# Batch 0's second round of attention visits as plain fp32 products with TensorE transposes, and the second parts of all weights made by GpSimd

## The chip, the cores and the metric

The kernel runs on one core of one Trainium2 chip. The metric is the device time of one execution in microseconds. Three timed runs of the kernel before took 1231.63 to 1234.51 us, with a median of 1234.36 us. The profile shown here is of another execution, which took 1228.56 us; its span from the first to the last instruction is 1226.8 us.

## The reference

```python
scores = scale * np.matmul(q, k.transpose(0, 1, 3, 2))        # 8 batches, 8 heads, 576 x 64
thresh = np.max(scores, axis=-1, keepdims=True) - tau
scores = np.where(scores >= thresh, scores, -1000000000.0)
scores = scores - np.max(scores, axis=-1, keepdims=True)
attn = np.exp(scores)
attn = attn / (np.sum(attn, axis=-1, keepdims=True) + 1e-09)
x = np.matmul(attn, v)                                         # back to 4608 x 512
h = x @ w_in                                                   # 512 x 2048
g = h * (1.0 / (1.0 + np.exp(-h)))
return g @ w_out                                               # 2048 x 512
```

Attention keeps only the scores that lie within tau of the row's maximum. Its output, with the heads side by side, goes through two large products with a SiLU between them. All inputs are fp32 except the two weight matrices, which arrive as 64-bit floats and are taken apart into words on the chip.

## The kernel before, in words

**Tiles and visits.** The work of attention is cut into tiles of 128 query rows against all 576 keys. A visit is a pair of heads of one batch. For batches 1 to 7 a visit has 9 tiles and covers everything ("all"). Batch 0 is done in two rounds: four "low" visits of 4 tiles each cover 256 query columns (tiles 0 to 15), then, after 12 empty steps, four "high" visits of 5 tiles each cover the other 320 (tiles 28 to 47). Batch 1 begins with tile 49, and the last tile is number 300. One step of the main loop handles one tile and, as a credit allows, one or more units of the two large products ("MoE units" below).

**What a tile does.** `scores` makes the products into PSUM (two buffers of two banks). `soft1` takes the negated maximum on VectorE (L458), `soft1b` the exponential on ScalarE (L468), `soft2` masks and sums on VectorE (L477). `soft2b` multiplies by the reciprocal, and `soft3` brings the tile into the transposed form that the product with v needs.

**Two ways of doing that.** The split way (all visits but the low ones) cuts every operand in two parts so that products of reduced precision add up to fp32: `split_k` (L360 ScalarE, L362 GpSimd), `split_q` (for batch 0 L345 and L346 on ScalarE and L347 on GpSimd, for the others L351 on ScalarE and L352 on VectorE) and `split_v` (L312, L313). A tile's scores are then four matmuls (L448), eight for the tile that two heads share. The scaling is on ScalarE (L495); GpSimd makes two 16-bit parts (L506, L509, L512; up to tile 35 the first one is on ScalarE, L504), a DMA transpose carries them over (L522), and `av` runs 28 16-bit matmuls for each half of a visit (L537). The direct way (the low visits) uses unsplit fp32 q, k and v: two fp32 matmuls a tile (L436, each of them two records in the profile), scaling on GpSimd (L491), five TensorE transposes (L393, L395), two ScalarE copies out of PSUM (L403, L404) and ten fp32 matmuls a visit (L413, two records each).

**The weights.** `load_weights` and `decode_weights` bring in w_in and w_out, 16 tiles each, and rebuild fp32 values (L191 ScalarE, L194 and L197 VectorE). When all 16 tiles of a matrix are decoded a common scale is found, and `split_weights` makes two 16-bit parts: for w_in by GpSimd scaling (L226), a ScalarE copy (L229) and a GpSimd subtraction (L230); for w_out by one ScalarE pass (L221) and one VectorE pass (L222).

**MoE units.** An h unit is 12 matmuls (L580) with a post on ScalarE and VectorE (L588, L589, L595, L596); an o unit is 12 matmuls (L611), four of them to an output tile. Batch 0's units come in two groups, of 256 columns after the low visits and of 320 after the high ones; later batches bring two groups of 288. A group may start only when the attention outputs of all four visits are there. The o units need all of w_out's parts.

**What sets the order.** The Python loop records instructions with priorities (`W_PLAN`, `PRI_*`), and a scheduler that runs when the program is built puts each engine's instructions into one fixed order. On the chip every engine, and the SyncE queue that issues the DMAs, goes through its order without overtaking. Where a group of MoE units stands between two tiles is therefore fixed, whatever the actual times are.

## Time and profile before

| what | value |
|---|---|
| median of 3 timed runs | 1234.36 us |
| profiled execution, its own time | 1228.56 us |
| its span | 1226.8 us |
| first score maximum of tile 28 (first high tile) | 73.38 us |
| first score maximum of tile 49 (batch 1) | 171.70 us |
| first score maximum of tile 95 | 324.32 us |
| TensorE / VectorE / ScalarE / GpSimd busy over the span | 93% / 76% / 66% / 60% |

A tile's place in time is read from its maximum (L458): there is one for each tile, in order, so the 17th is tile 28, the 37th is tile 49 and the 83rd is tile 95. In windows of the trace the clock column is the mean share of full speed that was granted to TensorE. A row of the timeline holds neighbouring instructions of one line, with the start of the first and the time to the end of the last; since matmuls are pipelined, the cost of a row on TensorE is the distance to the start of the next row. Line numbers are those of the kernel before.

### The profile page before, as it was taken

The numbers are of one execution on the slowest core, as the hardware profiler recorded it, in microseconds if no ns is written. First come the engines' busy times: TensorE is split into PE (matmuls) and PEld (weight loads), VectorE is DVE, ScalarE is ACT, GpSimd is POOL, SyncE is SP. The second block draws the span as 40 slices with busy tenths as digits, with TensorE's granted clock in tenths as the row PEclk, the third lists the DMA queues.
The fourth block names the chain that finished last, engine by engine and source line by source line (L and its number), as shares of the span: only waits on it lengthen the run. The fifth ranks groups of instructions, "written<-read, shape, count | busy, mean of one in ns | idle before, by whom it ended". The sixth has DMA issues, their size and how long they took to land.

```text
span 1226.8 us, 26991 instructions
## 1 busy us (share of the span) xinstructions
PE 1145.4 (93%) x9422; PEld 898.1 (73%) x9422; DVE 934.2 (76%) x2619; ACT 808.6 (66%) x1491; POOL 739.4 (60%) x936
## 2 busy tenths in 40 slices
PE   6867679999799999999999999999999999999998
PEld 4545458777677777877777877787778877777777
DVE  6988998987888988988889958887789848332330
ACT  5768876776777767776777747776678747333331
POOL 2289968786778778886888528872778447100000
PEclk9967889999999999999999999999999999999999
DMA  9659658687677777786896447872797346200000
GB/s 296 192 182 235 136 117 171 146 139 148 138 145 144 166 148 145 147 160 149 146 174 141 110 115 138 156 144 82 137 159 150 75 86 113 50 11 15 16 11 25
DMA packets 363480, 158.16 MB, mean 129 GB/s; under 512 B 329552, under 2 KB 338256, under 8 KB 363344
## 3 DMA queue, kind: packets, MB, share of 16 engines
q1 hardware_dynamic: 363344, 156.43, 60.6%
q8 instruction: 75, 1.23, 0.4%
q14 instruction: 61, 0.50, 0.1%
HBM read 66.72 MB, written 9.44 MB: 62 GB/s over the span
## 4 chain that ended last, share of the span: by engine, by line
PE 64%; DVE 16%; DMA 8%; ACT 5%; issue 3%; POOL 2%; SPq 1%; ACTq 0%; POOLq 0%; DVEq 0%
PE o L611 24%; PE h L580 22%; PE s L448 9%; PE a L537 7%; DVE w L477 4%; DVE sm L458 3%; DVE qstack L352 2%; DMA wT<-hl 2%; DMA vraw<-in_vL 2%; ACT w L468 2%; DMA wraw<-in_w_out 2%; ACT w L495 1%; DVE gbuf L596 1%; DMA kd<-in_kT 1%; DVE wst L222 1%
## 5 line engine op out<-in xcount | busy, mean ns | idle before, releaser
L580 PE MATMUL h<-x,wst 128*128 128x288 f16 (+2 forms) x3072 | 429.7, 289 | 15.6 <-DVE gbuf L596 12.0
L611 PE MATMUL o<-gbuf,wst 128*128 128x288 f16 (+2 forms) x3072 | 420.0, 286 | 2.0 <-ACT wst L621 1.9
L580 PEld LDWEIGHTS <-wst 128*128 128x128 f16 x3072 | 292.7, 99 | 105.3 <-issue 26.7
L611 PEld LDWEIGHTS <-wst 128*128 128x128 f16 x3072 | 292.8, 98 | 83.4 <-issue 6.7
L509 POOL TENSOR_TENSOR hl<-w,hl 128x512 f16<-128x512 f32 x272 | 326.4, 1200 | 14.6 <-ACT hl L504 1.2
L506 POOL TENSOR_SCALAR hl<-w 128x576 f16<-128x576 f32 x264 | 179.9, 684 | 202.5 <-ACT w L495 141.2
L468 ACT ACTIVATE w<-s,sm 128x576 f32<-128x576 f32 x288 | 210.9, 737 | 78.9 <-DVE sm L458 33.1
L477 DVE SCALAR_TENSOR_TENSOR w<-s,sm,w 128x576 f32<-128x576 f32 x288 | 232.6, 813 | 35.9 <-ACT w L468 34.0
L458 DVE TENSOR_REDUCE sm<-s 128x1 f32<-128x576 f32 x288 | 215.1, 751 | 41.5 <-PE s L448 32.4
L495 ACT ACTIVATE w<-w,sm 128x576 f32<-128x576 f32 x272 | 205.7, 770 | 49.3 <-DVE sm L485 47.1
L589 DVE SCALAR_TENSOR_TENSOR h<-th,h 128x288 f32<-128x288 f32 (+2 forms) x256 | 116.5, 457 | 109.3 <-ACT th L588 107.2
L588 ACT ACTIVATE th<-h,msc 128x288 f32<-128x288 f32 (+2 forms) x256 | 126.8, 498 | 106.4 <-PE h L580 104.7
L448 PE MATMUL s<-khi,qstack 128*128 128x288 f32 x608 | 160.0, 345 | 27.1 <-DVE w L477 23.4
L595 ACT ACTIVATE gbuf<-h 128x288 f16<-128x288 f32 (+2 forms) x256 | 103.6, 407 | 80.7 <-DVE h L589 79.7
L596 DVE SCALAR_TENSOR_TENSOR gbuf<-h,gbuf 128x288 f16<-128x288 f32 (+2 forms) x256 | 115.4, 453 | 40.1 <-ACT gbuf L595 39.1
L448 PEld LDWEIGHTS s<-khi,qstack 128*128 128x128 f32 x608 | 97.4, 196 | 51.3 <-issue 34.4
L448 PE MATMUL s<-klo,qstack 128*128 128x288 f32 x608 | 133.6, 301 | 0.0
L537 PE MATMUL a<-wT,v 128*64 128x288 f16 (+1 forms) x1680 | 129.7, 293 | 4.0 <-DMA wT<-hl 3.7
L362 POOL TENSOR_TENSOR klo<-kraw,khi 128x576 fp32r<-128x576 f32 x64 | 94.8, 1481 | 43.1 <-ACT khi L360 43.0
L537 PEld LDWEIGHTS <-v 128*64 128x64 f16 x1680 | 92.0, 111 | 31.5 <-issue 22.8
L512 POOL TENSOR_TENSOR hl<-w,hl 128x64 f16<-128x64 f32 x272 | 102.5, 377 | 0.0
L448 PEld LDWEIGHTS s<-klo,qstack 128*128 128x128 f32 x608 | 101.0, 195 | 0.3
(103 smaller groups left out, 831.6 us busy)
## 6 DMA issues: line engine op xcount, KB each, us to landing
qraw<-in_qT SPq DMA_DIRECT2D x128, 144.0 KB, 3.0
kraw<-in_kT SPq DMA_DIRECT2D x128, 144.0 KB, 3.0
vraw<-in_vL SPq DMA_DIRECT2D x32, 320.0 KB, 3.3
wraw<-in_w_out SPq DMA_DIRECT2D x16, 512.0 KB, 4.1
out_t<-wst SPq DMA_DIRECT2D x56, 144.0 KB, 2.2
wT<-hl SPq DMA_TRANSPOSE x304, 3.3
gbuf<-in_w_in SPq DMA_DIRECT2D x8, 512.0 KB, 7.1
wraw<-in_w_in SPq DMA_DIRECT2D x8, 512.0 KB, 6.5
```

What stands on the lines that cost most here:

```text
L448: nc.tensor.matmul(s_ps[:, j, :HALF], lhs, kk[:, j * HALF : (j + 1) * HALF], start=(n == 0), stop=(n == len(seq) - 1),)
L458: nc.vector.tensor_reduce(out=negm, in_=s_ps[:, :, :HALF], op=ALU.max, axis=AX.XY, negate=True)
L468: nc.scalar.activation(wtile[t].rearrange("p (j c) -> p j c", j=2), sps[t][:, :, :HALF], AF.Exp, bias=small[t][:, 0:1],)
L477: nc.vector.scalar_tensor_tensor(out=w3, in0=s_ps[:, :, :HALF], scalar=sm[:, 1:2], in1=w3, op0=ALU.is_ge, op1=ALU.mult, accum_out=sm[:, 2:3],)
L495: nc.scalar.activation(w, w, AF.Copy, scale=r)
L506: nc.gpsimd.tensor_scalar(out=fl[:, 0:S], in0=w, scalar1=1.0, scalar2=1.0, op0=ALU.mult, op1=ALU.mult)
L509: nc.gpsimd.tensor_tensor(out=fl[:, 640:1152], in0=w[:, 0:512], in1=fl[:, 0:512], op=ALU.subtract)
L537: nc.tensor.matmul(a_ps[odd * D : (odd + 1) * D, :n], vt[:, lo_v, odd, kv, :], wT[v, b * H + 2 * p + odd][:, kw, c0 - base : c0 - base + n ...
L580: nc.tensor.matmul(ph[:, :n], wi(c, f, lo_w), x16[b, lo_x][:, c, c0 : c0 + n], start=(k == 0), stop=(k == 11),)
L588: nc.scalar.activation(th[:, :n], ph[:, :n], AF.Tanh, scale=moe_sc[b][:, 0:1])
L596: nc.vector.scalar_tensor_tensor(out=g[:, 1, :n], in0=ph[:, :n], scalar=2.0**-14, in1=g[:, 0, :n], op0=ALU.mult, op1=ALU.subtract,)
L611: nc.tensor.matmul(ps[:, :n], wo(f, d, lo_w), g[:, lo_g, :n], start=(f == 0 and k == 0), stop=(f == NF - 1 and k == 2),)
```

## The change

The high visits of batch 0 now go the direct way too. Their q halves are loaded straight into two more zero-padded tiles, so that batch 0 needs no `split_q`, `split_k` or `split_v` and no DMA transposes. Their transposes use PSUM bank 1 and the bank that the product with v uses; the first group's MoE units take banks 0 and 2. `split_weights` handles w_out as w_in: GpSimd scales, ScalarE copies, GpSimd subtracts. Batch 1's v is loaded and its maximum taken later, and its scale is found four steps later.

```diff
     def split_weights(i):
-        if i >= 4 * NK:
-            nc.scalar.activation(hi, w, AF.Copy, scale=sc)
-            nc.vector.scalar_tensor_tensor(
-                out=w16[:, i, 512:1024], in0=w, scalar=sc, in1=hi, op0=ALU.mult, op1=ALU.subtract
-            )
-            return
         nc.gpsimd.tensor_scalar(
             out=w, in0=w, scalar1=sc, scalar2=1.0, op0=ALU.mult, op1=ALU.mult
         )
...
     def vscale(b):
         vsc[b] = pow2_scales(
-            vmx[b], f"v{b}", (None, 2)[b] if b < 2 else 0, squared=(b == 0)
+            vmx[b], f"v{b}", (None, 1)[b] if b < 2 else 0, squared=(b == 0)
         )
...
     def split_q(h, tiles):
-        if h < H:
-            nc.scalar.activation(src, src, AF.Copy, scale=gate)
-            nc.scalar.activation(dst, src, AF.Copy)
-            nc.gpsimd.tensor_tensor(
-                out=dst[D:P, :], in0=src[D:P, :], in1=dst[D:P, :].bitcast(F32), op=ALU.subtract
-            )
-        else:
-            nc.scalar.activation(dst, src, AF.Copy, scale=gate)
...
+    qzero = {}
+    for kind, base, n in (("low", 4096, 256), ("high", 5120, 320)):
...
     def load_direct(v):
+        qt = qzero[kind, v % 2]
+        n = VISITS[kind][2][0][1]
+        c0, c1 = (0, S - n) if kind == "low" else (S - n, 0)
+        nc.sync.dma_start(out=qt[0:D, 0:n], in_=qT[b, 2 * p, :, c0 : c0 + n])
+        nc.sync.dma_start(out=qt[D:P, n : 2 * n], in_=qT[b, 2 * p + 1, :, c1 : c1 + n])
...
     def soft3_direct(t):
-        main = bank([P, 4, P], f"tm_{t}")
+        main = bank([P, 4, P], f"tm_{t}", None if low else 1)
...
-        last = bank([P, P], f"tl_{t}")
+        if low:
+            last = bank([P, P], f"tl_{t}")
+        else:
+            last = ps_a.tile([P, 512], F32, tag="a", name=f"tl_{t}")[:, 0:P]
...
     def moe_units(b, c0, n):
+        if b == 0 and c0 == 0:
+            return h_units(b, c0, n, (0, 2)) + o_units(b, c0, n, (0, 2))
...
-        if kind == "low":
+        if b == 0:
             at(u - LOAD, lambda v=v: load_direct(v))
             at(u - 2, lambda v=v: scale_direct(v))
...
             if b == 0:
                 at(-4, lambda p=p: load_v(0, p))
                 at(0, lambda p=p: vmax(0, p))
-                at(V_SLOT + p, lambda p=p: split_v(0, p))
+            elif b == 1:
+                at(u + 5 * p - 20, lambda p=p: load_v(1, p))
+                at(u + 5 * p - 15, lambda p=p: vmax(1, p))
+                at(u + 9 * p + 4, lambda p=p: split_v(1, p))
...
-        at(u - 2 if b else 1, lambda b=b: vscale(b))
+        at((1, u + 2)[b] if b < 2 else u - 2, lambda b=b: vscale(b))
```

The order of instructions moves with it. Two places matter below. The first is GpSimd around tiles 41 to 43. In the rows, w32_41 is tile 41's weights after the exponential, hl its two 16-bit parts, klo the second part of k, and wst the MoE weights. Before, GpSimd stood there in the middle of the high tiles:

```order
L509 TENSOR_TENSOR hl_41_1935<-w32_41_1886,hl_41_1935 128x512
L512 TENSOR_TENSOR hl_41_1935<-w32_41_1886,hl_41_1935 128x64
L506 TENSOR_SCALAR hl_42_1983<-w32_42_1925 128x576
L509 TENSOR_TENSOR hl_42_1983<-w32_42_1925,hl_42_1983 128x512
L512 TENSOR_TENSOR hl_42_1983<-w32_42_1925,hl_42_1983 128x64
L362 TENSOR_TENSOR klo_8_2110<-kraw_8_8_2030,khi_8_2108 128x576
```

Now, from tile 38 on, one scaling pass stands for each tile (L488, the former L491), and w_out's scaling (L218, the former L226) and subtractions (L222, the former L230) stand between them:

```order
L488 TENSOR_SCALAR w32_38_1660<-w32_38_1660,sm_38_1659 128x576
L218 TENSOR_SCALAR wst_89<-wst_89,o_w_sc_1020 128x512 x15
L222 TENSOR_TENSOR wst_89<-wst_89 128x512
L218 TENSOR_SCALAR wst_89<-wst_89,o_w_sc_1020 128x512
L222 TENSOR_TENSOR wst_89<-wst_89 128x512
L488 TENSOR_SCALAR w32_39_1712<-w32_39_1712,sm_39_1711 128x576
L488 TENSOR_SCALAR w32_40_1749<-w32_40_1749,sm_40_1748 128x576
L222 TENSOR_TENSOR wst_89<-wst_89 128x512 x2
L488 TENSOR_SCALAR w32_41_1795<-w32_41_1795,sm_41_1794 128x576
```

A tile's three passes have become one, and all sixteen scalings of w_out stand in one row ahead of tile 39's.

The second place is TensorE around tile 85, where batch 2's attention begins. Before, pieces of batch 0's second group of o units (o_0_256) stood between the tiles' scores:

```order
L448 MATMUL s_85_3616<-khi_16_3549,qstack0_85 128x288 x2
L448 MATMUL s_85_3616<-klo_16_3551,qstack0_85 128x288 x2
L611 LDWEIGHTS wst_89
L611 MATMUL o_0_256_2_3594<-gbuf_61,wst_89 128x320
L448 MATMUL s_86_3653<-khi_16_3549,qstack0_85 128x288 x2
L448 MATMUL s_86_3653<-klo_16_3551,qstack0_85 128x288 x2
```

Now the scores of tiles 84 to 89 follow each other with nothing between (L445 is the former L448):

```order
L445 MATMUL s_84_3461<-khi_15_3203,qstack1_87 128x288 x2
L445 MATMUL s_84_3461<-klo_15_3205,qstack1_87 128x288 x2
L445 MATMUL s_85_3514<-khi_16_3435,qstack0_85 128x288 x2
L445 MATMUL s_85_3514<-klo_16_3437,qstack0_85 128x288 x2
L445 MATMUL s_86_3551<-khi_16_3435,qstack0_85 128x288 x2
L445 MATMUL s_86_3551<-klo_16_3437,qstack0_85 128x288 x2
L445 MATMUL s_87_3582<-khi_16_3435,qstack0_85 128x288 x2
L445 MATMUL s_87_3582<-klo_16_3437,qstack0_85 128x288 x2
```

All of batch 0's MoE units now stand ahead of tile 82: the whole first group of o units (192 matmuls) between the scores of tiles 49 and 51, where before none of them stood, and the second group between tiles 51 and 82. From there to tile 95 only 18 MoE matmuls stand on TensorE beside attention's own, where before 230 stood (146 of batch 0's o matmuls and 84 of batch 1's h matmuls).

More of the change, by code (lines that the diff above doesn't have):

```diff
@@ L366, in attention_moe @@
     direct = {}
[L367 to L371 removed]
+    qzero = {}
+    for kind, base, n in (("low", 4096, 256), ("high", 5120, 320)):
+        for i in range(2):
+            t = gbuf.bitcast(F32)[:, base + 2 * n * i : base + 2 * n * (i + 1)]
+            nc.gpsimd.memset(t[0:D, n : 2 * n], 0.0)
+            nc.gpsimd.memset(t[D:P, 0:n], 0.0)
+            qzero[kind, i] = t
     def load_direct(v):
[L374 removed]
+        b, p, kind = visits[v]
         kt = sb.tile([P, S], F32, tag="kraw", name=f"kd_{v}", bufs=2)
         nc.sync.dma_start(out=kt, in_=kT[b, 2 * p : 2 * p + 2].rearrange("h d s -> (h d) s"))
[L377 to L379 removed]
+        qt = qzero[kind, v % 2]
[3 more added lines that the diff above has]
+        nc.sync.dma_start(out=qt[D:P, n : 2 * n], in_=qT[b, 2 * p + 1, :, c1 : c1 + n])
         direct[v] = qt, kt
@@ L383, in scale_direct @@
         for j in range(2):
-            own = direct[v][0][j * D : (j + 1) * D, 256 * j : 256 * (j + 1)]
+            n = VISITS[visits[v][2]][2][0][1]
+            own = direct[v][0][j * D : (j + 1) * D, n * j : n * (j + 1)]
             nc.scalar.activation(own, own, AF.Copy, scale=gate[j * D : (j + 1) * D, :])
@@ L433, in scores @@
             qt, kt = direct[v]
-            o = (h % 2) * 256 + i * P
+            if visits[v][2] == "low":
+                o = (h % 2) * 256 + i * P
+            else:
+                o = (h % 2) * 384 + (i - 2) * P
             for j in range(2):
@@ L502, in soft3 @@
         fl = hl.rearrange("p j c -> p (j c)")
[L503 to L508 removed]
+        nc.gpsimd.tensor_scalar(
+            out=fl[:, 0:S], in0=w, scalar1=1.0, scalar2=1.0, op0=ALU.mult, op1=ALU.mult
+        )
         nc.gpsimd.tensor_tensor(
@@ L644, in moe_units @@
         if held:
-            for pair in zip(h_units(b, c0, n, (0, 1)), o_units(*held.pop(), 2)):
+            for pair in zip(h_units(b, c0, n, (0, 1)), o_units(*held.pop(), (2,))):
                 out.extend(pair)
```

31 lines of the change are left out of this document (8 added, 23 removed).

## The prediction

> **What bounds the kernel now.** I read the windows of the trace by stage first, cut at the score maxima (L458) of tiles 28, 49, 51 and 95; the timeline rows are those of tiles 28, 49, 82 and 95:
>
> ```profile
> 73.38 0.74 DVE L458 TENSOR_REDUCE sm<-s 128x1 f32<-128x576 f32 x1
> 171.70 0.75 DVE L458 TENSOR_REDUCE sm<-s 128x1 f32<-128x576 f32 x1
> 274.18 0.76 DVE L458 TENSOR_REDUCE sm<-s 128x1 f32<-128x576 f32 x1 [0.33 <-PE s L448]
> 324.32 0.75 DVE L458 TENSOR_REDUCE sm<-s 128x1 f32<-128x576 f32 x1
> ...
> core 0: us, PE busy (x) PEld busy (x) DVE busy (x) ACT busy (x) POOL busy (x), PEclk, DMA share, GB/s
> 0.00:73.40 73.40, 53.33 (x296) 34.89 (x296) 57.41 (x179) 47.50 (x90) 21.97 (x31) 0.91 0.77 238
> 73.40:171.70 98.30, 67.66 (x425) 49.75 (x426) 91.15 (x218) 80.01 (x147) 85.33 (x88) 0.74 0.70 172
> 171.70:179.70 8.00, 5.45 (x31) 4.07 (x29) 7.44 (x26) 5.12 (x10) 4.75 (x7) 0.57 0.51 105
> 179.70:324.30 144.60, 134.29 (x1128) 105.26 (x1125) 122.60 (x350) 102.59 (x181) 113.59 (x144) 1.00 0.78 151
> 324.30:500.00 175.70, 166.77 (x1431) 132.17 (x1430) 155.22 (x449) 130.83 (x239) 136.17 (x175) 1.00 0.73 146
> 500.00:1042.30 542.30, 536.78 (x4621) 427.85 (x4619) 449.01 (x1290) 384.10 (x701) 372.02 (x487) 1.00 0.67 132
> ```
>
> After 500 us TensorE is busy 99% of the time at full clock: the kernel is bound by TensorE there, and from 180 us on nearly so. Only ahead of tile 49 is it not. In the high stage (tiles 28 to 49, 98.3 us) VectorE is busy 93%, while TensorE idles for 30.6 us and runs at 0.74 of its clock. So any work added to TensorE is paid at the end, unless time is won in which TensorE now idles or is slowed. The forecast is that balance: work added, lost time recovered, lost time made anew.
>
> Next come the groups of the high stage.
>
> ```profile
> L197 DVE SCALAR_TENSOR_TENSOR wst<-wraw,wst 128x512 int32<-128x512 int32 x12 | 15.2, 1265 | 0.1
> L222 DVE SCALAR_TENSOR_TENSOR wst<-wst,o_w_sc 128x512 f16<-128x512 f32 x14 | 13.6, 993 | 0.0
> L313 DVE SCALAR_TENSOR_TENSOR v<-vraw,v_sc,v 128x640 f16<-128x640 f32 x3 | 3.8, 1254 | 0.0
> L495 ACT ACTIVATE w<-w,sm 128x576 f32<-128x576 f32 x18 | 13.8, 771 | 0.4 <-DVE sm L485 0.3
> L230 POOL TENSOR_TENSOR wst<-wst 128x512 f16<-128x512 f32 x16 | 19.5, 1241 | 0.1
> L362 POOL TENSOR_TENSOR klo<-kraw,khi 128x576 fp32r<-128x576 f32 x8 | 12.0, 1505 | 2.3 <-ACT khi L360 2.3
> L226 POOL TENSOR_SCALAR wst<-wst,i_w_sc 128x512 f32<-128x512 f32 x12 | 9.9, 843 | 0.0
> L491 POOL TENSOR_SCALAR w<-w,sm 128x576 f32<-128x576 f32 x2 | 2.1, 1036 | 0.0
> L580 PE MATMUL h<-x,wst 128*128 128x256 f16 (+1 forms) x160 | 24.9, 304 | 7.7 <-DVE gbuf L596 6.8 <-DVE sm L481 0.9
> ```
>
> L222 and L313, the passes that the change removes from VectorE, are 17.4 us of its 91.15. That speaks for a gain. What replaces them goes to GpSimd, which is already busy for 85.33 us.
>
> **Work added to TensorE.** Prices come from timeline rows at full clock, as the distance to the next row.
>
> ```profile
> 48.98 2.52 PE L413 MATMUL a<-wT,vraw 128*64 128x256 f32 x18
> 51.43 1.24 PE L436 MATMUL s<-kd,gbuf 128*128 128x288 f32 x4
> 52.50 0.62 PE L209 MATMUL wps<-wst 128*128 128x128 bf16 x8
> 52.96 0.60 PE L393 MATMUL tm<-ident,w 128*128 128x128 f32 x4
> 53.40 0.27 PE L395 MATMUL tl<-ident,w 128*128 128x128 f32 x1
> 53.51 1.14 PE L436 MATMUL s<-kd,gbuf 128*128 128x288 f32 x4
> ...
> 137.13 1.47 PE L580 MATMUL h<-x,wst 128*128 128x256 f16 x12 [1.82 <-DVE gbuf L596]
> 138.53 1.14 PE L537 MATMUL a<-wT,v 128*64 128x320 f16 x14
> 139.60 0.54 PE L448 MATMUL s<-khi,qstack 128*128 128x288 f32 x2
> ...
> 247.75 0.54 PE L448 MATMUL s<-khi,qstack 128*128 128x288 f32 x2
> ...
> 248.39 3.43 PE L580 MATMUL h<-x,wst 128*128 128x320 f16 x24
> ```
>
> A split tile's scores, two rows of which the second is left out, cost 0.64 us (247.75 to 248.39), the shared tile's twice that, and half a visit's product with v 2 x 1.07 = 2.14. The four high visits thus cost 16 x 0.64 + 4 x 1.28 + 4 x 2.14 = 24 us of full-clock work. The direct way costs 1.1 us for a tile's scores (51.43 to 52.50 is 1.07), 0.55 for its five transposes (52.96 to 53.51), and for a visit's product 20 records of (2.45/18) x 320/256 = 0.17, so 3.4: 20 x 1.65 + 4 x 3.4 = 47 us. TensorE gets **23 us more**; the records with 320 columns and single gaps could make it 20 to 27, I take 24.
>
> The Trainium skill, in "TensorE: Matmul & The Clock Gate", Part 4 (PE-mode transpose), gives about 275 ns for one 128x128 transpose inside a kernel, which would make the hundred new ones 27 us instead of 11 and the sum 16 us higher. The rows above show four in 0.44 us, 0.11 each, since they follow each other; the measurement decides.
>
> **The low stage.** Batch 0's split_v leaves VectorE (4 x 1.25, with two of batch 1's maxima, less two q parts), and ScalarE and GpSimd no longer hold the low tiles for high q and k. VectorE is the busiest engine there (57.41 of 73.40), and TensorE idles for 20 us. I take **-5 us**; 0 if the weights' loads pace it, -8 at best.
>
> **The high stage.** VectorE: 91 less 13.6, 3.8, two q parts (1.6) and three maxima (2.4), plus 8 more post passes of 0.42, so 73 us. ScalarE: 80 less the scalings (13.8) and the 16-bit copies, k, q and v work (19 together), plus twenty times the two copies out of PSUM (under 0.9 together) and some posts: about 70. GpSimd must, from the first scaling of w_in to tile 49, go through 32 scalings of weights, 32 subtractions, 21 tile scalings and 2 k parts: 32 x 0.843 + 32 x 1.241 + 21 x 1.04 + 2 x 1.5 = 91 us. It begins here:
>
> ```profile
> 69.94 2.19 POOL L226 TENSOR_SCALAR wst<-wst,i_w_sc 128x512 f32<-128x512 f32 x3 [3.28 <-DVE i_w_sc L146]
> ```
>
> With the low stage's 5 us that is 65, so GpSimd is the new bound of the stage and ends at 156 without a wait; with 3 us of waits (for the ScalarE copy between scaling and subtraction, and for w_out's scale, where tiles 39 and on are queued behind the sixteen scalings) tile 49 comes at 159. The stage, from 68 to 159, takes 91 us.
>
> TensorE's full-clock work in it before: 160 h matmuls at 1.40/12 (18.7), 20 tiles of split scores (15.4), three visits' products (6.4), and some 7 of weight maxima and the last low visit: 47, so 51 of 98.3 us were lost. After, by the order: 20 direct tiles' scores (22), 95 transposes (10.5), 40 + 20 product records (9.5), 192 h matmuls (22.4), 4 of weight maxima: 68, so 23 of 91 are lost. Recovered: **28 us**. Between tiles 49 and 51 now stands the o block; TensorE is full there, where 8 us held 4 of work: **-2**.
>
> **What is lost anew.** The order lets batch 0's MoE units run out early. From tile 82 to 95 there is attention alone, and it is paced by the engines behind it, whose prices are those of 500 to 600 us:
>
> ```profile
> L509 POOL TENSOR_TENSOR hl<-w,hl 128x512 f16<-128x512 f32 x31 | 38.3, 1234 | 2.3
> L506 POOL TENSOR_SCALAR hl<-w 128x576 f16<-128x576 f32 x32 | 21.4, 669 | 19.9 <-ACT w L495 17.4 <-ACT th L588 2.5
> L512 POOL TENSOR_TENSOR hl<-w,hl 128x64 f16<-128x64 f32 x31 | 11.7, 378 | 0.0
> ...
> L477 DVE SCALAR_TENSOR_TENSOR w<-s,sm,w 128x576 f32<-128x576 f32 x30 | 24.2, 815 | 4.0 <-ACT w L468 3.9
> L458 DVE TENSOR_REDUCE sm<-s 128x1 f32<-128x576 f32 x32 | 23.9, 751 | 1.8 <-PE s L448 1.7
> ```
>
> GpSimd needs 1.234 + 0.669 + 0.378 = 2.28 us a tile and 0.3 for k; VectorE 1.57 for the two large passes, some 0.6 for the small ones and 0.5 for q, v and maxima: 2.6 to 2.8 us either way, 36 us for 13 tiles. TensorE's work in it is 13 tiles' scores (9.6), one visit's product (4) and 18 MoE matmuls: 15. So 21 us are lost; before, the same tiles took 50 us (274.18 to 324.32), with 230 MoE matmuls for the 18, so 29 us more of work: 6 lost. **+15** (13 to 18). Tiles 51 to 57 are a smaller case: VectorE has six tiles and, moved there, four split_v and five maxima, some 21 us, against 13 of TensorE work; before, 2 were lost. **+6**. From tile 57 to 82, and after 95, TensorE is full as before: -1.
>
> **The sum**, against the profiled execution's own 1228.6 us (1.8 around its span): 24 - 5 - 28 - 2 + 15 + 6 - 1 = **+9 us**, 1237.6. The median shown lies 5.8 us above that execution, so I predict **1243 us**. The price of the transposes and of the direct products is read from the low stage; the least certain term is the stage's length, where 10% is 9 us.
>
> **Rivals.**
> *GpSimd is quick, and it is faster.* L197 costs 0.68 us in the low stage and 1.265 here, so VectorE and GpSimd stretch each other, and VectorE will do less. With the shortest rows of the stage,
>
> ```profile
> 84.68 0.68 POOL L226 TENSOR_SCALAR wst<-wst,i_w_sc 128x512 f32<-128x512 f32 x1
> 39.50 0.68 DVE L197 SCALAR_TENSOR_TENSOR wst<-gbuf,wst 128x512 int32<-128x512 int32 x1
> ```
>
> and 1.14 for the subtraction, GpSimd has 77 us and ends at 142 to 146; the stage loses 10 instead of 23, and the lull at 2.4 us a tile loses 4 less: -8 us, 1226. It decides once the subtraction's mean is under 1.15 us. Against it: GpSimd's load does not fall.
> *The lull is given back, and nothing changes.* The tiles run ahead in it, and in 324 to 500 us TensorE still idles 8.9 of 175.7. If all of that is filled: 0 to +1 us, 1235. Against it: the two PSUM buffers let a tile run only one ahead on TensorE.
> *The clock stays low, and it is much slower.* If the high stage keeps the granted 0.74, 68 us of work take 92, more than the 91 that GpSimd asks for, and with half of the former idle time (15) the stage takes 107: +25 us, 1259. It decides once the clock is under 68/91 = 0.75. For it: 0.57 between tiles 49 and 51 with TensorE 68% busy. Against it: the low stage's second half, at 90% busy with such transposes in it, was at full clock:
>
> ```profile
> 40.00:60.00 20.00, 17.90 (x123) 12.21 (x122) 18.30 (x53) 12.69 (x26) 5.96 (x7) 1.00 0.60 184
> ```
>
> The same Part 4 says that transposes do not count as activity for the clock gate, which would speak for this rival; this row does not bear it out.
>
> **How the numbers follow.** The forecast has 0.45 (its own range 1236 to 1252), the quick GpSimd 0.25, the lull given back 0.15, the low clock 0.15. About 0.3% (3.7 us) is what a measurement of this kernel can tell from no change. Slower takes the low clock and nine tenths of the forecast, 0.55; within it the lull and a tenth of the forecast, 0.20; faster 0.25. The range reaches to most of both sides: 1224 to 1260.
>
> **What would show it.** Tile 49's maximum near 159 us, with GpSimd over 90% busy ahead of it and the clock near 0.9; tile 95's near 335, later than the 324.32 of before though tile 49's is earlier; TensorE idle over half of the time between tiles 84 and 92. If tile 49 comes before 147 or the lull's tiles take under 2.4 us each, the kernel is faster and I am wrong; if TensorE's busy time in the stage is near 90 us at a clock under 0.8, the third rival holds.

## The result, and the profile after

Four runs of the changed kernel took 1249.29 to 1251.13 us, median 1249.75; four of the kernel before on the same chip had a median of 1233.43. The ratio is **1.0152, 95% interval 1.0128 to 1.0175**: the change makes the kernel 1.5% slower, where the forecast was 1243 us. The profiled execution took 1249.85 us and its span is 1248.1. The before profile, 1228.56 us, lies below all of its timed runs, so that the two profiled executions differ by 21.3 us and the medians by 16.3; the stages below are compared between the profiles.

The windows of the changed kernel, cut at the maxima of tiles 28, 49, 51, 57, 82 and 95, then the two parts of the stage from 28 to 49, cut at tile 33. The columns are those of the windows in the prediction.

```profile
0.00:72.60 72.60, 52.27 (x301) 34.24 (x302) 55.41 (x175) 44.36 (x84) 16.59 (x30) 0.93 0.76 235
72.60:164.60 92.00, 73.66 (x479) 52.15 (x479) 69.93 (x192) 65.96 (x147) 76.97 (x84) 0.91 0.28 87
164.60:192.00 27.40, 27.40 (x239) 22.74 (x238) 4.63 (x16) 5.79 (x15) 4.89 (x7) 1.00 0.08 25
192.00:215.50 23.50, 14.50 (x84) 9.54 (x82) 22.99 (x57) 16.36 (x30) 12.25 (x14) 0.80 0.77 172
215.50:300.70 85.20, 80.88 (x651) 60.58 (x651) 73.36 (x217) 60.27 (x106) 65.42 (x84) 0.97 0.69 138
300.70:338.30 37.60, 21.57 (x132) 16.71 (x131) 31.93 (x89) 24.40 (x41) 30.25 (x39) 0.69 0.85 169
500.00:1063.60 563.60, 551.78 (x4740) 440.42 (x4738) 463.48 (x1333) 393.97 (x721) 385.20 (x501) 1.00 0.68 131
...
72.60:103.30 30.70, 19.53 (x95) 11.33 (x95) 22.82 (x50) 16.73 (x31) 26.49 (x29) 0.72 0.53 169
103.30:164.60 61.30, 54.13 (x387) 40.82 (x385) 47.10 (x143) 49.23 (x117) 50.48 (x56) 1.00 0.16 45
```

Tile 49 now comes at 164.6 us instead of 171.7, 7 us early. By tile 51 the kernel is 12 us behind (192.0 against 179.7), by tile 82 26 us (300.7 against 274.2), and at tile 95 14 us (338.3 against 324.3). Two of the rows are stretches in which TensorE is idle and slowed: 23.5 us with 14.5 busy at a clock of 0.80, and 37.6 us with 21.57 busy at 0.69. The kernel before took 17.4 and 50.1 us for the same tiles (51 to 57, and 82 to 95), at full clock and filled with MoE matmuls:

```profile
179.70:197.10 17.40, 16.55 (x150) 14.35 (x148) 15.93 (x43) 12.18 (x23) 15.61 (x20) 1.00 0.79 156
274.20:324.30 50.10, 44.43 (x371) 34.43 (x369) 40.16 (x116) 32.72 (x57) 35.07 (x43) 1.00 0.80 157
```

To set the added work apart from the idle time, I count for each kernel the matmuls that stand in each stretch of TensorE's order, at the prediction's prices at full clock, and call the rest of the stretch lost: idle time, and what a halved clock costs. The sum of the work is 1101 us before and 1125 after. The prices hold in the changed kernel's rows at full clock (18 product records in 2.98 us, a tile's scores in 0.98 to 1.07), but the 24 us are a count at these prices. Counting by start times instead of by the order moves most entries by less than 2 us and some, above all from 51 to 82, by up to 4.5.

| lost time, us | to 28 | 28–33 | 33–49 | 49–51 | 51–57 | 57–82 | 82–95 | after 95 | all |
|---|---|---|---|---|---|---|---|---|---|
| before | 34.2 | 15.6 | 37.1 | 4.0 | 1.7 | 4.8 | 6.0 | 22.8 | 126 |
| after | 32.8 | 18.2 | 7.4 | -0.5 | 11.1 | 7.3 | 23.0 | 24.1 | 123 |

So 33 us of lost time are recovered up to tile 51, 27 of them between tiles 28 and 49, and 30 are lost anew behind it. What stays is the work added, 24 us, less the difference of 3.

### The profile page after: what moved, and what is told of

The parts are those of the page before. It is cut to its first block, busy times and chain, and to the rows that moved or that the text cites. A ratio compares the mean times of both kernels' runs of the same rounds, so it can differ in the third digit from the quotient of the medians.

```text
span 1248.1 us, 26945 instructions
## 1 busy us (share of the span) xinstructions
PE 1160.0 (93%) x9474; PEld 905.3 (73%) x9474; DVE 916.5 (73%) x2599; ACT 792.9 (64%) x1491; POOL 722.1 (58%) x926
## 4 chain that ended last, share of the span: by engine, by line
PE 55%; DVE 16%; DMA 11%; POOL 7%; ACT 6%; issue 6%; SPq 0%; POOLq 0%; ACTq 0%; DVEq 0%
PE o L605 20%; PE h L574 18%; PE s L445 7%; PE a L531 6%; DMA wT<-hl 5%; DVE w L474 4%; DVE sm L455 3%; DVE qstack L337 2%; POOL hl L503 2%; DMA wraw<-in_w_in 2%; POOL hl L500 2%; ACT w L465 2%; DMA vraw<-in_vL 1%; DMA wraw<-in_w_out 1%; ACT w L492 1%
## 5 line engine op out<-in xcount | busy, mean ns | idle before, releaser
L574 PE MATMUL h<-x,wst 128*128 128x288 f16 (+2 forms) x3072 | 427.4, 288 | 12.5 <-DVE x L550 6.0
L503 POOL TENSOR_TENSOR hl<-w,hl 128x512 f16<-128x512 f32 x252 | 302.2, 1199 | 12.2
L500 POOL TENSOR_SCALAR hl<-w 128x576 f16<-128x576 f32 x252 | 170.6, 680 | 225.1 <-ACT w L492 158.9
L474 DVE SCALAR_TENSOR_TENSOR w<-s,sm,w 128x576 f32<-128x576 f32 x288 | 232.9, 813 | 55.7 <-ACT w L465 53.5
L492 ACT ACTIVATE w<-w,sm 128x576 f32<-128x576 f32 x252 | 190.8, 771 | 44.0 <-DVE sm L482 42.0
L445 PE MATMUL s<-khi,qstack 128*128 128x288 f32 x560 | 147.0, 344 | 19.1 <-DVE w L474 13.9
L531 PE MATMUL a<-wT,v 128*64 128x288 f16 x1568 | 118.2, 291 | 10.8 <-DMA wT<-hl 9.8
L445 PE MATMUL s<-klo,qstack 128*128 128x288 f32 x560 | 122.6, 300 | 0.0
L445 PEld LDWEIGHTS s<-khi,qstack 128*128 128x128 f32 x560 | 89.1, 194 | 39.6 <-issue 27.1
L347 POOL TENSOR_TENSOR klo<-kraw,khi 128x576 fp32r<-128x576 f32 x56 | 82.2, 1467 | 39.3 <-ACT khi L345 38.7
L506 POOL TENSOR_TENSOR hl<-w,hl 128x64 f16<-128x64 f32 x252 | 93.0, 369 | 0.0
L445 PEld LDWEIGHTS s<-klo,qstack 128*128 128x128 f32 x560 | 92.4, 193 | 0.5 <-issue 0.2
```

The source lines that it names most:

```text
L445: nc.tensor.matmul(s_ps[:, j, :HALF], lhs, kk[:, j * HALF : (j + 1) * HALF], start=(n == 0), stop=(n == len(seq) - 1),)
L474: nc.vector.scalar_tensor_tensor(out=w3, in0=s_ps[:, :, :HALF], scalar=sm[:, 1:2], in1=w3, op0=ALU.is_ge, op1=ALU.mult, accum_out=sm[:, 2:3],)
L492: nc.scalar.activation(w, w, AF.Copy, scale=r)
L500: nc.gpsimd.tensor_scalar(out=fl[:, 0:S], in0=w, scalar1=1.0, scalar2=1.0, op0=ALU.mult, op1=ALU.mult)
L503: nc.gpsimd.tensor_tensor(out=fl[:, 640:1152], in0=w[:, 0:512], in1=fl[:, 0:512], op=ALU.subtract)
L531: nc.tensor.matmul(a_ps[odd * D : (odd + 1) * D, :n], vt[:, lo_v, odd, kv, :], wT[v, b * H + 2 * p + odd][:, kw, c0 - base : c0 - base + n ...
```

## The experiments

All are compared with the kernel before in runs on the same chip. The order of the instructions is drawn anew for each of them, as it was for the change. Two terms come back: RATES holds the credit for each tile with which batch 0's first and second group of MoE units are drawn, and W_PLAN[0] the steps at which w_in is loaded, scaled and split.

### One part of the change alone

**e1_direct_only** is the change without its second part: w_out's second parts are made by VectorE again.

```diff
         sc = wsc["in" if i < 4 * NK else "out"][:, 0:1]
+        if i >= 4 * NK:
+            nc.scalar.activation(hi, w, AF.Copy, scale=sc)
+            nc.vector.scalar_tensor_tensor(
+                out=w16[:, i, 512:1024], in0=w, scalar=sc, in1=hi, op0=ALU.mult, op1=ALU.subtract
+            )
+            return
```

> The change without its second half: the high visits go the direct way, but w_out's second parts are made by VectorE again, with the ScalarE pass ahead of them. In its order the o units of the first group no longer stand in one block ahead of tile 51 and the stretch with little MoE work is shorter (tiles 85 to 95 hold 1.9 us of TensorE work a tile, against 1.0 to 1.3 in the change). Theory (added TensorE work, plus stretches in which MoE work has run out): TensorE work is as in the change, about half of the lull's 21 us goes, VectorE has 15 us back in the high stage; 1240 us, 1235 to 1246, so between the two kernels. Rival (the weights' move is what helps, the direct visits alone are worse): above 1250 us.

Measured: 1239.25 us (1236.28 to 1241.7), ratio 1.0068 (1.0042 to 1.0095). Two of its windows, tiles 28 to 49 and 82 to 95:

```profile
72.40:167.40 95.00, 73.51 (x458) 50.48 (x458) 79.84 (x205) 66.96 (x144) 53.14 (x55) 0.89 0.27 85
...
294.40:336.70 42.30, 32.48 (x230) 24.65 (x228) 35.08 (x102) 28.04 (x49) 29.77 (x40) 0.88 0.74 151
```

GpSimd has 53.14 us to do in the high stage instead of 76.97, and the stage is not shorter but 3 us longer (95.0). Its length does not follow GpSimd's load, against the prediction. (VectorE, which makes w_out's second parts here, has 10 us more to do, 79.84 instead of 69.93.) The kernel is nevertheless 10 us faster than with the whole change, and that comes from elsewhere: here 189 of the 192 o matmuls stand between tiles 51 and 57, not in one block ahead of 51, and that stretch loses nothing (-0.9 against 11.1); 82 to 95 loses 13.9 against 23.0.

**e2_weights_only** is the kernel before with the other part: the five lines of `split_weights` that take w_out to ScalarE and VectorE are removed.

```diff
-        if i >= 4 * NK:
-            nc.scalar.activation(hi, w, AF.Copy, scale=sc)
-            nc.vector.scalar_tensor_tensor(
...
-            return
```

> The kernel before with the second half of the change alone: w_out's second parts by GpSimd, the high visits split as before. No TensorE work is added, VectorE loses 15 us of its 91 in the high stage, GpSimd gains 33 on top of its 85. Theory: GpSimd then has to hold 118 us in a stage of 98, so tile 49 comes 5 to 15 us later than 171.7 and the time is 1236 to 1246 us. Rival (VectorE is what bounds the high stage, and taking L222 from it is worth its length): tile 49 near 157 us, 1219 to 1224 us.

Measured: 1239.67 us, ratio 1.0088 (1.0052 to 1.0125). The time is inside the theory's band, but for another reason. Tiles 28 to 49 and 51 to 57:

```profile
70.60:171.10 100.50, 71.46 (x475) 53.42 (x476) 81.89 (x213) 77.50 (x147) 96.62 (x106) 0.79 0.65 158
...
179.70:202.60 22.90, 14.11 (x105) 10.42 (x104) 15.78 (x46) 15.53 (x26) 22.90 (x28) 0.93 0.67 129
```

GpSimd is indeed full in the high stage (96.62 of 100.5), yet tile 49 is not later than before (171.1 against 171.7). The 234 MoE matmuls that the order now puts ahead of tile 47 (139 before) are missing later: tiles 51 to 57 take 22.9 us instead of 17.4, with GpSimd busy in every microsecond of it and TensorE for 14.11, and lose 11.3.

### Is it the lull?

**e3_slow_rate** is the change with smaller credits, so that batch 0's units last longer.

```diff
-RATES = (1.3, 0.8)
+RATES = (0.6, 0.6)
```

> The change with the rates at which MoE units are handed out in batch 0 set to 0.6 and 0.6 instead of 1.3 and 0.8, nothing else. All work is the same; only the order moves: the o units are spread over tiles 49 to 60 and MoE work lasts to about tile 88 instead of 82. By the order and the change's own prices the stretches with less than 2.7 us of TensorE work a tile lack 11 us in all instead of 26. Theory: 10 to 15 us are won back against the change, 1235 to 1240 us, with tile 49 as in the change (164 us, within 3) and tile 95 some 12 us earlier than 338. Rival (the tiles' run ahead is repaid later, so the lull costs nothing): 1248 to 1251 us.

Measured: 1234.29 us (1229.83 to 1239.32), ratio 1.0021 (1.0001 to 1.0041), 15.5 us faster than the change by the medians and 16 by the two ratios (the runs were on different chips), just under the theory's band. Its windows from 28 to 33, 51 to 57 and 82 to 95:

```profile
71.20:102.60 31.40, 19.40 (x96) 11.27 (x95) 23.70 (x50) 16.39 (x30) 26.02 (x28) 0.72 0.49 163
...
169.40:197.80 28.40, 27.57 (x237) 23.12 (x236) 25.21 (x64) 18.35 (x34) 16.58 (x18) 1.00 0.75 160
281.40:325.20 43.80, 34.11 (x263) 25.94 (x261) 36.04 (x106) 29.18 (x52) 32.46 (x43) 0.88 0.73 149
```

Tile 49 stays where it was (162.6 us), tiles 51 to 57 hold 237 matmuls instead of 84 and lose 3.0 instead of 11.1, and 82 to 95 loses 14.7 instead of 23.0. The place of batch 0's MoE units behind tile 49 is thereby shown to cost the change nearly all that it is slower by.

**e4_direct_slow** is e1 with these credits, **e5_before_slow** the kernel before with them, as the control for the credits by themselves.

```diff
 # both
-RATES = (1.3, 0.8)
+RATES = (0.6, 0.6)
```

> Both of the other two edits together: direct high visits, w_out's second parts on VectorE as before, rates of 0.6 and 0.6. In its order there is hardly a stretch without MoE work (3 us lacking). Theory: the added TensorE work of 23 us remains, and what the high stage recovers is set against it alone: 1228 to 1236 us, within 0.4% of before. Rival (the direct visits cost more than their TensorE work, for instance by the clock or by waits): above 1240 us.

> The kernel before with the rates of batch 0 set to 0.6 and 0.6, nothing else: the control for the two runs with that edit. Before, hardly any stretch lacks MoE work, and the edit makes the order a little worse (7 us lacking in all instead of 4). Theory (the rate helps only where MoE work runs out): 1230 to 1237 us, the same as before or 3 us more. Rival (the lower rate is worth something by itself, and the direct visits are not): 1222 to 1227 us.

Measured: e4 1226.54 us, ratio 0.9968 (0.9946 to 0.9989); e5 1229.33 us, 0.9986 (0.9972 to 1.0000); they lie 1.5 and 0.7 us under their theories' bands. Their windows from 82 to 95, e4 first:

```profile
276.60:318.80 42.20, 37.63 (x307) 27.99 (x302) 33.33 (x94) 28.20 (x48) 32.84 (x42) 0.98 0.82 169
```

```profile
277.60:318.40 40.80, 37.55 (x307) 27.87 (x306) 34.63 (x94) 27.58 (x47) 31.62 (x41) 1.00 0.88 176
```

With the same 307 matmuls in both, the lull is gone (5.8 and 5.1 us lost). The credits alone give the kernel before a tenth of a per cent; they give the direct visits 12.7 us (1239.25 to 1226.54). Without the lull the direct visits are worth some 0.2 to 0.3% against either kernel, which is within an order's own scatter: e4 and its variants e8 to e10 lie between 0.9968 and 1.0009.

### What paces the high stage?

If GpSimd does not, TensorE's own work or its clock may. **e6** and **e7** are e3 with the four main transposes of each high, or each low tile, made twice into the same place. The output stays what it was; TensorE gets 80 x 0.11 = 8.8 us and 64 x 0.11 = 7 us more to do.

```diff
 # e6_transposes_twice_high; e7 the same with "if not low"
-        for k in range(4):
+        for k in range(4) if low else (0, 1, 2, 3, 0, 1, 2, 3):
```

> The change with the rates of 0.6 and 0.6, and the four main transposes of each of the 20 high tiles made twice, into the same place: 80 more transposes, 8.8 us of TensorE work at 0.11 us each, with nothing else to do for any engine. Theory (TensorE work added to the high stage is paid at the end): 5 to 9 us more than with the rates alone, 1239 to 1243 us against 1234. Rival (the high stage has idle TensorE time that takes it): 1232 to 1236 us.

> The same doubling in the 16 low tiles instead: 64 more transposes, 7 us of TensorE work, in a stage in which TensorE idles for 20 us of 73. Theory (it is paid only where TensorE is full): 0 to 2 us more than with the rates alone, 1232 to 1237 us. If it costs 6 us or more, TensorE work is paid anywhere, and the low stage is on the path through its transposes.

Measured: e6 1230.98 us, ratio 1.0013 (0.9997 to 1.0028), a miss; e7 1222.48 us (1218.5 to 1228.24), ratio 0.9936 (0.9912 to 0.9960), another miss, on the fast side. e6 from tile 33 to 49, then e7 from 28 to 33:

```profile
101.20:167.80 66.60, 61.72 (x468) 49.55 (x467) 48.46 (x148) 51.01 (x120) 53.62 (x59) 1.00 0.15 44
```

```profile
68.50:95.50 27.00, 19.43 (x111) 12.64 (x110) 23.84 (x51) 16.36 (x32) 24.33 (x25) 0.81 0.51 173
```

e6 does pay in the stage: tile 49 comes at 167.8 instead of 162.6. But its new order also puts more MoE matmuls there. From tile 33 to 49 it holds 64 transposes and 31 MoE matmuls more than e3, some 11 us of work, and takes 6.6 us more; the lost time falls from 7.4 to 2.5. So from tile 33 on TensorE paces most of the stage, not all of it. The 5.2 us are then given back behind tile 49, in part because those MoE matmuls no longer stand there; that 82 to 95 loses 9.6 instead of 14.7 was not explained. In e7 the added work is hidden, as expected, but tiles 28 to 33 take 27.0 us instead of e3's 31.4, at a clock of 0.81 instead of 0.72. The prediction did not look at that stretch by itself.

### Tiles 28 to 33

There the kernels with direct high visits shown so far, e7 apart, took 30 to 32 us, with TensorE busy for less than two thirds of it; in the changed kernel and e3 the clock was 0.72. The waits of TensorE in that stretch of the changed kernel (total us, times, longest), and the timeline of its GpSimd:

```profile
PE wps L207 <- DVE wst L195: 10.3, 6, 3.8
```

```profile
72.37 12.37 POOL L218 TENSOR_SCALAR wst<-wst,i_w_sc 128x512 f32<-128x512 f32 x15
...
88.42 3.34 POOL L488 TENSOR_SCALAR w<-w,sm 128x576 f32<-128x576 f32 x4
```

TensorE stands behind the transposes of w_out's maxima (wps), which wait for the decoding by VectorE, and behind them in its order are the last low visit's product and the first h units. And GpSimd goes through fifteen scalings of w_in in one row before it comes to the tile scalings at 88.42. Either of the two can be the cause. The chain of work that ended last, from 66 to 103.3 us, speaks for the first:

```profile
by line: DMA wraw<-in_w_out 31.6%; PE a L407 16.3%; DVE wst L195 9.4%; PE s L433 8.6%; issue 8.1%; ACT wst L189 5.3%; DVE sm L455 4.9%; ACT w L465 3.7%; PE h L574 2.3%; PE tm L384 2.0%; PE wps L207 1.6%; DVE sm L458 1.4%; DVE msc L285 1.3%;
```

It runs through the loads of w_out and their decoding, and the burst is not on it. Nor do the loads run freely: from 60 to 104 us those of w_out wait for 33.9 us, put down to VectorE's decoding of earlier tiles.

**e8_gap4** is e4 with 4 instead of 12 empty steps ahead of tile 28, so that fewer decodings stand there.

```diff
-GAP, GAP1 = 12, 1
+GAP, GAP1 = 4, 1
```

> Direct visits, w_out's second parts on VectorE, rates of 0.6 and 0.6, and 4 empty steps instead of 12 between the low and the high visits. The high tiles are handed out earlier against w_out's decoding and the first h units; in the order MoE work never runs out (1 us lacking) and more of it stands ahead of tile 49 (130 us of TensorE work instead of 101). Theory: no lull is left in either, so the time is that of the run with 12 steps within 4 us, 1223 to 1230 us, unless the high stage itself gets shorter. Rival (w_out's decoding paces the stage's first 30 us, and an earlier start lets the tiles queue behind it): 1232 us or more, with tiles 28 to 33 still taking about 30 us.

Measured: 1231.61 us, ratio 1.0009 (0.9990 to 1.0028), between the two expectations; tiles 28 to 33 take 30.3 us instead of e4's 32.0. It settles nothing.

**e9_win_late** is e4 with w_in's loads spread up to step 12 instead of 10, its scaling at step 12 and its split up to step 18.

```diff
-W_PLAN = ((0, 0, 10, 13, 0), (16, 9, 22, 26, 150))
+W_PLAN = ((0, 0, 12, 18, 0), (16, 9, 22, 26, 150))
```

> Direct visits, w_out's second parts on VectorE, rates of 0.6 and 0.6, and w_in's split handed out over steps 12 to 18 instead of 10 to 13. In its order GpSimd scales tile 15's weights ahead of the burst of 15 w_in scalings (12 us) instead of behind it, so that the last low visit's product and the first h units stand further ahead on TensorE (behind 23 of w_out's 32 maximum groups instead of 27). Theory (in tiles 28 to 33 TensorE waits because that burst holds back tile 15, and the clock halves in the gap): these five tiles take 25 to 29 us instead of 32, with less than 10 us of halved clock; the order has more lull (10 us lacking instead of 3), so the time is 1224 to 1231 us. Rival (w_out's loads pace these tiles): still 31 us or more, 1230 to 1236 us.

Measured: 1230.79 us, ratio 0.9994 (0.9977 to 1.0012). The start of its GpSimd's burst, and its window from 28 to 33:

```profile
74.46 0.74 POOL L494 TENSOR_SCALAR w<-w,sm 128x576 f32<-128x576 f32 x1 [7.39 <-PE s L439]
...
79.11 12.56 POOL L224 TENSOR_SCALAR wst<-wst,i_w_sc 128x512 f32<-128x512 f32 x15 [3.90 <-DVE i_w_sc L144]
```

```profile
70.00:97.60 27.60, 17.71 (x120) 11.08 (x118) 23.02 (x66) 14.53 (x28) 19.24 (x22) 0.93 0.54 174
```

The tile's scaling now stands ahead of the burst (in e4 the burst began at 71.84 with the tile behind it), the wait for decoding falls from 8.8 to 3.8 us over the same window, the clock is 0.93 and the stretch takes 27.6 us: 4.4 less than e4. That the edit shortens the slow stretch is shown; by what is not, since three things moved at once: the burst, the loads of w_in, and the place of the last low visit's product and the first h unit on TensorE, which now stands behind 92 transposes of w_out's maxima instead of 108. The chain still runs through w_out's loads (47.6% from 66 to 98 us), which speaks against the burst as the cause by itself. The gain is not kept: 82 to 95 loses 14.2 us here instead of e4's 5.8, in another order.

**e10_transposes_twice_low_direct** asks whether e7's gain comes back without GpSimd's part of w_out: e4 with the low tiles' transposes made twice (the edit of e7).

```diff
-        for k in range(4):
+        for k in range(4) if not low else (0, 1, 2, 3, 0, 1, 2, 3):
```

> Direct visits, w_out's second parts on VectorE, rates of 0.6 and 0.6, and the four main transposes of each of the 16 low tiles made twice, as in the run in which this took 12 us off. Theory A (more TensorE activity in the low stage keeps the clock up in tiles 28 to 33): it again takes 5 us or more off, 1215 to 1221 us, with tiles 28 to 33 at 27 us. Theory B (the earlier gain came from the order, which each edit draws anew): by the order's lull (5 us lacking instead of 3) 1224 to 1230 us.

Measured: 1228.74 us, ratio 0.9985 (0.9972 to 0.9997). Tiles 28 to 33 take 26.8 us at a clock of 0.87, as with e7, but 57 to 82 then loses 11.4 us where e4 lost 7.1, and the time is no better than e4's. What the sixty-four more transposes do by themselves, and what the new order does (the first h unit stands behind 104 transposes of maxima instead of 108, for one), was not told apart. In both e7 and e10 GpSimd's burst begins at about 64.4 us, 6 to 7 us earlier than in e3 and e4 (70.9 and 71.8).

### A better version

**e11_half_weights** is e3 with w_out's second parts shared: odd tiles by VectorE, even ones by GpSimd.

```diff
+        if i >= 4 * NK and i % 2:
+            nc.scalar.activation(hi, w, AF.Copy, scale=sc)
+            nc.vector.scalar_tensor_tensor(
...
+            return
```

> Direct visits, rates of 0.6 and 0.6, and w_out's second parts made by VectorE for odd tiles and by GpSimd for even ones. In the order 6 us of lull lack, between 11 with all on GpSimd (1234 us) and 3 with all on VectorE (1226.5 us). Theory (the lull in the order sets the time): 1227 to 1233 us. Rival (neither VectorE nor GpSimd is then full in the high stage, and that stage gets shorter): tile 49 ahead of 158 us and 1222 us or less.

Measured: 1226.67 us, ratio 0.9971 (0.9956 to 0.9985). Tile 49 comes at 164.9 us, 2.3 later than in e3, yet 95 at 321.4 instead of 325.2. The time is just under the theory's band, and the rival's early tile 49 did not come.

**e12_together** adds a later w_in to e11 and sets the second credit back to 0.8, with which fewer tiles stand without MoE matmuls in the order.

```diff
-RATES = (0.6, 0.6)
+RATES = (0.6, 0.8)
-W_PLAN = ((0, 0, 10, 13, 0), (16, 9, 22, 26, 150))
+W_PLAN = ((0, 0, 11, 17, 0), (16, 9, 22, 26, 150))
```

> What the runs point to, together: direct visits, w_out's second parts on VectorE for odd tiles and on GpSimd for even ones, w_in's split handed out over steps 11 to 17 (tile 15's scaling then stands ahead of the burst, and the first h unit behind 22 of w_out's 32 maximum groups instead of 27), and rates of 0.6 and 0.8, with which the order lacks 3 us of MoE work instead of 6. Theory (lull and the tiles 28 to 33 add up): tiles 28 to 33 take under 29 us and the time is 1219 to 1226 us, faster than before and than half the weights alone (1226.7). Rival (each edit draws a new order whose other losses are as large as these gains): 1226 to 1233 us, the same as before.

Measured: 1222.37 us (1217.49 to 1225.84), ratio **0.9916 (0.9892 to 0.9939)**. It beats the kernel before by 0.8%, and by the two ratios the changed kernel by over 2%. Tiles 28 to 33, 33 to 49 and 82 to 95:

```profile
68.20:93.60 25.40, 17.86 (x115) 11.27 (x112) 22.44 (x61) 15.38 (x30) 19.73 (x23) 0.89 0.54 175
93.60:157.40 63.80, 53.92 (x347) 40.22 (x347) 55.11 (x149) 52.57 (x119) 47.48 (x48) 0.91 0.23 69
269.90:321.30 51.40, 44.73 (x339) 33.15 (x336) 35.40 (x106) 30.33 (x53) 33.43 (x45) 0.90 0.77 148
```

Tile 49 is at 157.4 us. The last row still loses 11 us, though 339 matmuls stand in it; what it waits for was not followed up.

Over all runs the length of tiles 28 to 33 goes with the number of maxima transposes ahead of the first h unit on TensorE: the seven kernels with 108 (the change, e1, e3, e4, e6, e8, e11) take 30 to 32 us, e7 and e10 with 104 take 27, the kernel before, e2 and e5 with 100 take 27, e9 with 92 takes 27.6, and e12 with 88 takes 25.4. No run moved that place alone.

The lost time of the kernels by the same count (without e8, which was not counted; the part after 95 is in the sums):

| lost time, us | to 28 | 28–33 | 33–49 | 49–51 | 51–57 | 57–82 | 82–95 | all | TensorE's work |
|---|---|---|---|---|---|---|---|---|---|
| before | 34.2 | 15.6 | 37.1 | 4.0 | 1.7 | 4.8 | 6.0 | 126 | 1101 |
| after | 32.8 | 18.2 | 7.4 | -0.5 | 11.1 | 7.3 | 23.0 | 123 | 1125 |
| e1 | 32.6 | 17.9 | 12.9 | 0.1 | -0.9 | 15.3 | 13.9 | 113 | 1125 |
| e2 | 31.5 | 15.2 | 32.3 | 3.7 | 11.3 | 11.2 | 7.8 | 137 | 1101 |
| e3 | 31.4 | 19.0 | 7.4 | -0.3 | 3.0 | 5.1 | 14.7 | 106 | 1125 |
| e4 | 31.3 | 19.5 | 9.4 | -0.4 | 5.5 | 7.1 | 5.8 | 101 | 1125 |
| e5 | 32.0 | 15.2 | 37.0 | 2.7 | 1.1 | 8.8 | 5.1 | 124 | 1101 |
| e6 | 30.4 | 18.6 | 2.5 | -0.5 | 1.0 | 7.2 | 9.6 | 93 | 1133 |
| e7 | 23.1 | 12.9 | 10.8 | 0.4 | -0.8 | 6.8 | 8.7 | 89 | 1132 |
| e9 | 32.0 | 14.8 | 14.6 | 0.1 | 0.8 | 5.5 | 14.2 | 106 | 1125 |
| e10 | 23.3 | 12.7 | 12.3 | 0.1 | 1.8 | 11.4 | 8.4 | 94 | 1132 |
| e11 | 30.6 | 18.0 | 12.4 | 0.1 | 0.9 | 3.8 | 10.8 | 96 | 1125 |
| e12 | 30.3 | 12.5 | 13.2 | 0.1 | 4.3 | 6.4 | 11.0 | 99 | 1125 |

Two columns carry the reading. In 33 to 49 every kernel with direct high visits loses 3 to 15 us and every one without them 32 to 37: that is what the direct visits give. In 82 to 95 the loss runs from 5 to 23 us with the same engines and the same arithmetic. The number of MoE units that the order leaves there explains the extremes and not the rest: e3, e6 and e7 hold nearly the same number of matmuls in it (263, 267 and 263) and lose 14.7, 9.6 and 8.7 us. In e7 and e10, 7 of the 8 us less in the first column are no gain: the doubled transposes are counted there as work and were hidden.

## Why the prediction was right, and where its terms were off

The time lies in the forecast's own range of 1236 to 1252 us, near its upper end. The forecast said slower, by a sum of +9 us over the profiled execution; by the same count +21.3 was measured. Some of these 12 us may belong to the profiled execution before, which lies 5.8 us under its median: by the medians the change cost 16.3 us where 8.6 were forecast. Term by term:

| term | predicted | measured |
|---|---|---|
| work added to TensorE | +24 | +24 (by count) |
| low stage, to tile 28 | -5 | -1.4 |
| high stage, tiles 28 to 49 | -28 | -27.1 |
| tiles 49 to 51 | -2 | -4.5 |
| tiles 51 to 57 | +6 | +9.4 |
| tiles 82 to 95 | +15 | +17.0 |
| tiles 57 to 82, and after 95 | -1 | +3.8 |

**The lull was right.** It was predicted that TensorE would idle from tile 82 to 95, for 36 us of which 15 are lost anew; it took 37.6 us and 17. The timeline of TensorE in the changed kernel shows how it goes:

```profile
303.50 0.51 PE L445 MATMUL s<-khi,qstack 128*128 128x288 f32 x2 [1.40 <-DVE sm L458]
303.84 0.43 PE L445 MATMUL s<-klo,qstack 128*128 128x288 f32 x2
308.45 0.82 PE L445 MATMUL s<-khi,qstack 128*128 128x288 f32 x2 [4.18 <-DVE w L474]
309.07 0.68 PE L445 MATMUL s<-klo,qstack 128*128 128x288 f32 x2
```

Nothing but score matmuls stands in these rows, and they wait for VectorE's masking (L474) to free a PSUM buffer. VectorE itself waits once, for a tile of v to land:

```profile
DVE vmx L265 <- DMA vraw<-in_vL: 3.2, 1, 3.2
```

That wait, up to 306.7 us, covers more than half of TensorE's gap of 4.18. Without it 34.4 us are left for 13 tiles, 2.65 each, inside the prediction's 2.6 to 2.8; with it a tile takes 2.89. VectorE is busy for 31.93 us, nearly all of what the wait leaves, and GpSimd for 30.25. So the lull was priced by the right engines, and the load is what the price lacked. One sign did not come: between tiles 84 and 92 TensorE was to be idle over half of the time and was busy for 14.94 of 20.2 us, at 0.65 of its clock. That the cause of the lull is the order is shown by e3, which changes the credits alone, and by e4.

**The high stage had the right length by luck.** 91 us were predicted and 92.0 measured; 28 us recovered and 27.1 measured. But the step "GpSimd is the new bound of the stage" fell. GpSimd was to be over 90% busy and was busy for 76.97 of 92.0 us, 84%:

```profile
L222 POOL TENSOR_TENSOR wst<-wst 128x512 f16<-128x512 f32 x31 | 36.8, 1200 | 7.4 <-ACT wst L221 7.3
L488 POOL TENSOR_SCALAR w<-w,sm 128x576 f32<-128x576 f32 x19 | 14.5, 767 | 7.6 <-DVE sm L482 4.4 <-DVE o_w_sc L144 2.1 <-DVE o_w_cl L118 1.1
L218 POOL TENSOR_SCALAR wst<-wst,o_w_sc 128x512 f32<-128x512 f32 x16 | 10.7, 694 | 0.0
```

These are the groups of that stage on GpSimd. A tile's scaling took 0.767 us where the prediction used 1.04, and w_out's scaling 0.694 for 0.843. Three errors cancelled: GpSimd was to begin at 65 us, work for 91 and wait for 3, so that tile 49 comes at 159; it began w_in's scalings at 72.4, worked for 77 and waited for 15, and tile 49 came at 164.6. What does pace the stage are two things in a row. In its first third (30.7 us, clock 0.72) TensorE waits for the maxima of w_out, and w_out's loads and decoding are on the chain; e9 and e12 shorten that part, and which of their moves does it is open. In the rest TensorE is busy for 54.13 of 61.3 us at full clock, and e6 shows that more work there makes it longer, by less than the work. GpSimd has a share in that: the row of w_out's scalings from 127.6 us on is 16.3% of the chain from 103.3 to 164.6, with TensorE busy beside it for 12.50 of 13.7 us. e1, with 24 us less for GpSimd and a stage 3 us longer, speaks against GpSimd as the bound, though VectorE has 10 us more there.

**The low stage was mis-sized.** The step "VectorE is the busiest engine there ... I take -5 us" failed: tile 28 is only 0.8 us earlier, though VectorE has 2 us less to do (55.41 for 57.41). The prediction named the case, "0 if the weights' loads pace it". The waits of ScalarE from 20 to 72.6 us of the changed kernel speak for that:

```profile
ACT wst L189 <- DMA wraw<-in_w_in: 5.2, 6, 1.0
ACT wst L189 <- DMA wraw<-in_w_out: 4.8, 5, 1.8
```

In the kernel before, from 20 to 73 us, they are smaller:

```profile
ACT wst L191 <- DMA wraw<-in_w_in: 3.5, 4, 1.4
ACT wst L191 <- DMA wraw<-in_w_out: 2.5, 4, 1.3
```

No experiment was made on it, so that this cause is argued and not shown.

**From tile 49 to 57 both terms were too small.** The block of 192 o matmuls ahead of tile 51 is there: TensorE is busy for 27.40 of 27.40 us, and the stretch gains 4.5 instead of 2. The 2 does not follow from the prediction's own figures: 8 us that held 4 of work, and then are full, give 4. Then tiles 51 to 57 have nothing left and take 23.5 us instead of 21, with VectorE busy for 22.99: the four split_v that moved there cost it 1.470 us each, where the prediction had them at 1.25. In e1, e3 and the later direct kernels most of these o units stand behind tile 51: the loss from 51 to 57 falls to between -0.9 and 5.5 us, while the gain from 49 to 51 stays.

**"From tile 57 to 82, and after 95, TensorE is full as before: -1" was the largest miss**, 4.8 us in all: 2.5 and 1.3 were lost instead. Most of the first is the tail of the gap ahead of it, whose halved clock lasts to 219.8 us:

```profile
215.50:219.77 4.27, 3.04 (x12) 1.72 (x12) 4.21 (x14) 3.86 (x8) 2.38 (x3) 0.50 0.29 82
219.77:300.70 80.93, 77.83 (x641) 58.86 (x639) 69.15 (x204) 56.41 (x98) 63.05 (x82) 1.00 0.71 141
```

Half the clock for 4.3 us is about 2 us of work. The prediction had the cost of the small lull end at tile 57, and gave the slowed clock behind a lull no term. The whole miss is also of the size that a new order moves (57 to 82 runs from 3.8 to 15.3 in the table).

**The rivals.** The quick GpSimd was to decide "once the subtraction's mean is under 1.15 us"; it is 1.200, and tile 49 came at 164.6, not before 147. The lull given back is refuted: after tile 95 the loss is 24.1 us, as before (22.8), and e3 gains 15.5 us by taking the lull away. The low clock was to decide under 0.75 in the high stage; it is 0.91 there, with full clock from tile 33 on. In the 30.7 us ahead of it, it is 0.72, so that this rival had a place but a third of the stage only.

**What stays open.** Each edit changes the order of everything behind it, and the totals of e8 to e11 lie within 5 us of each other for stretches that differ by up to 8. Which instruction's place makes e7 faster than e3 was not found, nor what shortens tiles 28 to 33 in e9 and e12, nor was the low stage's pacing tried by itself.

## What to carry to other kernels

Work moved to the bounding engine is paid for where that engine is full, while time won ahead of it is kept only if that engine finds something to do later: read in the written order where its filler now runs out, and price that stretch by the engines that then stand alone. When an edit redraws a static order, run a control that changes the order alone (here the credits), and spread the filler anew before judging the edit: the same change was 1.5% slower with the old credits and, with the filler respread, w_in's burst moved and w_out's second parts shared, 0.8% faster. An engine that is 84% busy in a stage of the right length is not yet its bound; taking a third of its work away is a cheap way to see, if the work does not land on another busy engine.
